# First block's reciprocals over two DMA queues, its second norm by DMA transpose, denominators of three blocks in one visit, and a new order

## The chip, the cores and the metric

The kernel runs on one core of a Trainium2 chip. The metric is the device time of one execution in microseconds (us). The core's engines run side by side, each in the order of its own instruction stream: TensorE (PE, matmuls, with its weight loads shown as PEld), VectorE (DVE), ScalarE (ACT), GpSimd (POOL) and SyncE (SP, which here issues DMAs). They wait for each other through semaphores.

## The reference

One transformer block on x of 2048 rows by 512 columns, bfloat16, without biases: a pre-norm linear attention with 32 heads of width 16, then a pre-norm MLP of width 1792 with ReLU.

```python
qkv = (layernorm(x) @ wqkv) split into q, k, v by head
phi = lambda t: where(t > 0, t + 1, exp(t)) + 1e-6
kv  = sum over s of phi(k)[s, d] * v[s, e]
z   = sum over s of phi(k)[s, d]
o   = (phi(q) @ kv) / (phi(q) @ z + 1e-6)
h   = x + o @ wo
out = h + relu(layernorm(h) @ w1) @ w2
```

## The kernel before, in words

Rows come in 16 tiles of 128 (index t, 0 to 15) and four blocks of four tiles (index c; "block 1" in this text is c = 0). Nothing is scheduled by a tool: `ORDER` is one long string of words, and the program reads it from left to right and records each word's instructions. So each engine's stream is the sequence of that engine's words, and only data and buffers make one engine wait for another. The eight PSUM banks are assigned in the words: in most of them the number behind the indices of the work is the bank.

The words that this text uses, with the engine of each:

- SP: `lx`, `lk`, `lq`, `lv`, `lo`, `l1`, `l2` load x, the three parts of wqkv, wo, w1 and w2; `X` and `x` turn a normalised tile by DMA transpose into lnT (first norm and second norm); `wb` writes a block's reciprocals to HBM (scr), and eight `rb` read them back spread over the partitions (rr); `fd` stores an output tile.
- DVE: `S` and `A` are the statistics of a tile of x, `N` its normalisation; `s`, `a`, `n` the same for h. `M` and `D` finish phi for k (`qM`, `qD` for q). `zc`, `zh` prepare z; `kx` masks kv; `mD` copies half of M (kv times wo) out of PSUM; `dm` multiplies phi(q) by the reciprocals; `hD` adds x; `pD` is the ReLU of two p blocks; `fo` finishes an output tile.
- ACT: `R` and `r` are the reciprocal deviations, `E` the copy of a tile turned by PE, `F` and `U` the exp and the ReLU of k (`qF`, `qU` of q), `gA` and `mA` copy the other halves of G and M, `dl4` and `dx4` take log and exp of the denominators (a reciprocal), `nA` normalises a tile of h.
- PE: `T` and `t` turn a tile by four transposes; `K`, `Q`, `G`, `h`, `p` are blocks of four 512-column matmuls; `ph` is half a p block; `kv` and `m` are small products; `d4` makes a block's denominators with four matmuls, one for each 32 partitions of a bank; `f` is half of the 14 matmuls of an output tile; `z` sums phi(k).

k and q come first (K and Q while x arrives), then G = x-norm times phi(k), which uses banks 4 to 7, then kv and M, and then for each block: denominators, `dm`, h, second norm, p, f. Tiles 0 to 4 of the first norm are turned by PE (`T`, `E`), the others by SP (`X`). In the second norm, tiles 2 and 3 are turned by PE (`t`, then a copy `v` on DVE), the others by SP (`x`).

Lines of the profile that matter: L214 to L220 loads, L248 to L262 statistics and norm, L287 transposes on PE, L297 `E`, L308 and L309 DMA transposes, L316 K, L324 Q, L334 and L337 exp and ReLU, L406 `gA`, L422 `kx`, L440 denominators, L471 spreads, L484 `dm`, L493 h, L508 and L517 p, L537 f.

Of the kernel before, what the change touches and what calls it, by code (L numbers as in the profile page):

```python
# [15 lines left out]


ORDER = """
table const masks warm.70.7.64 warm.2.7 lx.0.1 S.0 A.0 R.0.1 lx.1.1 S.1 lx.2.1 A.1 N.0 T.0.1 lk.0.4 S.2 R.1.1
N.1 T.1.2 lx.3.1 A.2 E.0 K.0.4 R.2.1 lx.4.2 S.3 N.2 T.2.1 E.1 A.3 S.5 R.3.1 K.1.0.0.2 K.1.0.2.2 N.3 S.4 A.5 A.4  # L20
E.2 T.3.2 K.2.6.0.2 K.2.6.2.2 F.0.1 M.0.1 lx.6.2 E.3 S.7 lq.0.4 R.4.2 lx.8.4 Q.0.3.1 N.4 U.0.1 A.7 F.1.1 F.2.1
T.4.2 N.5 S.6 Q.0.1.4 U.1.1 M.1.1 A.6 lx.12.4 M.2.1 D.0.1 R.6.2 K.3.7.0.2 K.3.7.2.2 E.4 X.5 U.2.1 U.3.1 D.1.1
N.6 Q.0.0.3 N.7 S.10 qF.0.0.2 K.4.5 K.5.6 S.8 A.10 S.9 A.8 qU.0.0.2 S.12 F.4.2 D.2.1 X.6 Q.0.2.0 A.9 A.12 K.6.2
S.13 S.11 M.4.2 A.11 A.13 U.4.2 D.4.2 F.3.1 R.8.2 N.9 M.3.1 X.7 K.7.3 R.12.2 R.10.2 N.8 F.6.2 D.3.1 N.13 S.15
G.0 G.1 U.6.2 S.14 X.9 X.8 N.10 A.14 A.15 N.12 qM.0.0.2 M.6.2 X.13 qF.0.2.2 R.14.2 qU.0.2.2 qM.0.2.2 N.11 G.2
G.3 G.5 G.4 N.14 X.12 K.9.3 K.8.2 K.13.1 N.15 qD.0.0.2 D.6.2 za.4.1 X.11 X.10 F.8.2 U.8.2 M.8.2 K.12.0 U.12.2
F.12.2 G.7 za.6.0 K.11.3 D.8.2 qD.0.2.2 M.12.2 za.8.0 K.10.2 F.10.2 X.14 G.8 K.14.0 U.10.2 X.15 K.15.1 M.10.2 zf
lv.2.2 lv.0.2 G.9 D.10.2 zhi D.12.2 F.14.2 G.6 G.10 G.11 M.14.2 zlo U.14.2 D.14.2 z.0.0 z.2.0 z.3.0 z.1.0 G.14
lo.0.2 lo.2.2 zc zh d4.0.1 dl4.0 l1.0.2 G.13 G.12 G.15 dx4.0 gA.2.2 Q.1.1.3 Q.1.0.2 qF.1.0.2 gD.0.2 kv.1.4
kv.3.4 kv.0.4 kv.2.4 kx qU.1.0.2 qM.1.0.2 qD.1.0.2 Q.1.3.1 Q.1.2.0 qF.1.2.2 m.0.2 m.1.3 mD.0.2 m.3.7 m.2.6 wb.0  # L30
Q.2.0.4 Q.2.1.5 rb.0.7 rb.0.1 rb.0.6 rb.0.3 rb.0.0 rb.0.2 rb.0.4 rb.0.5 l1.2.2 qM.1.2.2 qU.1.2.2 Q.2.3.1
qD.1.2.2 mA.2.2 qF.2.0.2 Q.2.2.0 qU.2.0.2 dm.0.2.2 dm.0.0.2 qM.2.0.2 h.1.6 hD.1 s.1 a.1 qU.2.2.2 d4.1.3 dl4.1
h.0.7 hD.0 s.0 dx4.1 h.2.6 h.3.5 a.0 l2.0.7 wb.1 hD.2 nA.1 hD.3 qF.2.2.2 nA.0 s.2 s.3 Q.3.0.2 Q.3.1.3 a.2
Q.3.3.6 a.3 qF.3.0.2 qU.3.0.2 Q.3.2.5 x.1 r.0.4 qF.3.2.2 n.2 t.2.7 n.3 t.3.4 qD.2.0.2 v.2 v.3 x.0 ph.0.3.1.0
ph.0.1.3.0 ph.0.2.0.0 ph.0.3.1.1 qM.2.2.2 qM.3.0.2 ph.0.0.2.0 ph.0.0.2.1 qM.3.2.2 qD.3.0.2 qU.3.2.2 qD.2.2.2
ph.0.2.0.1 qD.3.2.2 p.0.7.5 d4.2.6.2 pD.0.2.2 dl4.2 dl4.3 rb.1.4 rb.1.6 rb.1.3 rb.1.2 rb.1.0 rb.1.1 ph.0.1.3.1
rb.1.7 rb.1.5 p.0.6.4 dx4.2 dm.1.0.2 dm.1.2.2 h.4.0 pD.0.0.2 hD.4 pD.0.6.2 p.0.5.1 h.6.6 dx4.3 p.0.4.0 hD.6
l2.7.7 h.5.4 pA.0.4.2 s.4 s.6 hD.5 h.7.7 a.4 a.6 p.0.11.6 p.0.10.5 s.5 hD.7 a.5 p.0.9.4 wb.2 rb.2.6 n.4 rb.2.0
rb.2.4 s.7 n.6 rb.2.3 rb.2.2 rb.2.1 a.7 n.5 n.7 rb.2.5 rb.2.7 dm.2.0.2 dm.2.2.2 pD.0.10.2 p.0.13.1 p.0.12.0
p.0.8.3 pD.0.12.2 wb.3 r.4.4 rb.3.0 rb.3.4 h.10.7 hD.10 x.6 h.8.2 h.11.6 hD.8 s.10 rb.3.5 rb.3.1 rb.3.6  # L40
f.1.0.0.7 rb.3.3 rb.3.2 rb.3.7 s.8 hD.11 pD.0.8.2 h.9.5 f.3.1.0.7 x.7 x.5 s.11 a.8 hD.9 f.1.0.7.7 f.0.4.0.7 a.10
a.11 x.4 dm.3.2.2 dm.3.0.2 h.14.7 h.12.3 s.9 n.11 h.15.6 a.9 n.10 h.13.2 fo.1 n.9 n.8 hD.14 s.14 hD.12 x.11
hD.15 f.0.4.7.7 r.8.4 p.1.13.7 p.1.6.3 a.14 hD.13 s.12 s.15 s.13 a.12 a.15 a.13 n.14 p.1.12.6 n.13 f.3.1.7.7
n.12 n.15 p.1.2.5 fo.0 pD.1.12.2 x.10 p.1.7.4 fo.3 p.1.3.6 x.9 pD.1.6.2 pD.1.2.2 r.12.4 x.8 p.1.11.2 p.1.10.1
pD.1.10.2 f.2.4.0.7 p.2.0.6 p.2.1.7 f.2.4.7.7 pD.2.0.2 p.2.10.0 p.2.11.1 fo.2 x.14 p.2.6.2 p.2.7.3 x.15 fd.3
p.2.13.7 p.2.12.6 pD.2.10.2 pD.2.6.2 x.12 fd.1 pD.2.12.2 p.2.2.0 x.13 fd.0 p.2.3.1 p.1.5.6 p.1.4.5 pD.2.2.2
pD.1.4.2 p.1.0.3 p.1.1.4 p.1.9.1 p.1.8.0 pD.1.0.2 pD.1.8.2 f.4.4.0.7 f.4.4.7.7 fo.4 fd.4 f.5.3.0.7 f.5.3.7.7
fo.5 fd.2 f.6.7.0.7 f.6.7.7.7 fo.6 p.2.4.2 p.2.5.3 f.7.0.0.7 f.7.0.7.7 pD.2.4.2 fo.7 p.3.6.1 p.3.7.2 pD.3.6.2
p.3.8.3 p.3.9.4 p.3.5.1 pD.3.8.2 p.3.4.0 pD.3.4.2 fd.6 p.3.10.3 p.3.11.4 pD.3.10.2 p.3.2.0 p.3.3.1 p.3.0.5
p.3.1.6 pD.3.2.2 pD.3.0.2 p.3.13.3 fd.7 p.3.12.2 pD.3.12.2 f.10.1.0.7 f.15.2.0.14.3.1 f.15.7.0.14.0.2 p.2.8.4  # L50
p.2.9.5 fo.15.3.1 fd.15.3.1 fo.15.0.2 pD.2.8.2 f.8.7.0.7 f.10.1.7.7 fo.10 f.8.7.7.7 fo.8 f.14.2.0.7 f.14.2.7.7
f.13.3.0.7 fd.5 fd.8 fd.10 fo.14 f.13.3.7.7 fo.13 f.9.0.0.7 f.9.0.7.7 fd.15.0.2 f.11.6.0.7 f.11.6.7.7 fd.13 fo.9
f.12.0.0.7 fd.9 f.12.0.7.7 fo.11 fd.14 fd.11 fo.12 fd.12 f.15.2.0.14.2.1 fo.15.2.1 fd.15.2.1
"""


# [1 line left out]
def kernel(  # L58
# [10 lines left out]
    nc = tc.nc  # L69
# [3 lines left out]
    S, D = xf.shape  # L73
# [7 lines left out]
    KD = D // P  # L81
    KF = FF // P
# [5 lines left out]
    const = ctx.enter_context(tc.tile_pool(name="const", bufs=1))  # L88
# [58 lines left out]
    rb = big.tile([P, NE, 2, CW], BF16, name="rb")  # L147
# [10 lines left out]
    def pk(t, n=1):  # L158
        return pk_lo[:, t : t + n, :] if t < 2 else acts[0][:, t - 2 : t - 2 + n, :]
# [9 lines left out]
    z_on = lambda n: z_sb.rearrange("p (k o) -> p k o", o=1).broadcast_to([P, KD, n])  # L169
    at_bank = {}  # L170
    summed, stated = set(), set()
    dsts = {"k": lambda t, n: pk(t, n), "q": lambda i, n: pqT[i // KD][:, i % KD : i % KD + n, :]}
    unit = {"k": 0, "q": NT}

# [137 lines left out]
    def op_K(t, b, k=0, n=KD):  # L312
        c, j = divmod(t, CT)
        at_bank["k", t] = b
        for kd in range(k, k + n):
            nc.tensor.matmul(  # L316
                bk[:, b, :], lhsT=lnT[c][:, kd, j * P : (j + 1) * P], rhs=wk_sb[:, kd, :],
                start=(kd == 0), stop=(kd == KD - 1),
            )

    def op_Q(c, j, b):
# [145 lines left out]
    def op_wb(c):  # L467
        nc.sync.dma_start(out=scr[c].rearrange("j h o n -> (j h) (o n)"), in_=rd[:, c, :])

    def op_rb(c, h):  # L470
        nc.sync.dma_start(  # L471
            out=rr[h * DH : (h + 1) * DH, :, :],
            in_=scr[c][:, h, :, :].rearrange("j o n -> o j n").broadcast_to([DH, KD, CW]),
        )

    def op_rs(c, j):
        rows = rd[j * Q4 : j * Q4 + P // DH, c, :]
        nc.sync.dma_start(
            out=rr[:, j, :], in_=rows.rearrange("h (o n) -> h o n", o=1).broadcast_to([P // DH, DH, CW])
        )  # L480
# [52 lines left out]
    def op_f(t, b, f0, n, k=0, w=KD):  # L533
        c, j = divmod(t, CT)
        at_bank["f", t, k] = b
        for f in range(f0, f0 + n):
            nc.tensor.matmul(  # L537
                bk[:, b, 0 : w * P], lhsT=acts[c % 2][:, f, j * P : (j + 1) * P],
                rhs=w2_sb[:, f, k * P : (k + w) * P],
                start=(f == 0), stop=(f == KF - 1),  # L540
            )

    def op_fo(t, k=0, w=KD):
# [44 lines left out]
```

## Time and profile before

| What | Value |
|---|---|
| Median of 3 runs | 169.78 us (169.41 to 170.17) |
| Profiled execution, span from first to last instruction | 168.0 us |
| What the median has beyond that span | 1.8 us |
| PE busy | 162.7 us (97%) |
| DVE, ACT, POOL busy | 115.6, 49.5, 4.8 us |
| Granted TensorE clock | 1.00 |
| DMA, mean | 95 GB/s |

The profile gives no other time of the profiled execution than its span; it starts with the program's first instruction and ends with its last, and what the runs' times have beyond it is launch and end. Busy is the time in which an engine works; matmuls are pipelined, so that the length of a single one, or of a short group, contains about 0.17 us of draining that the next one overlaps. A row of the timeline gives start, length, engine, line, operation, what is written and read, and in brackets the idle time of the engine ahead of it with what ended it. A row of SP is the issue of a DMA alone: its data moves later.

### The profile page before, as it was taken

What the parts mean: (1) busy time and instruction counts of PE and PEld (TensorE: products, weight loads), DVE (VectorE), ACT (ScalarE), POOL (GpSimd) and SP (SyncE); (2) the same over time, 40 slices, a digit from 0 to 9 for tenths busy, and PEclk for the clock granted to TensorE, in tenths of its full rate; (3) what the DMA queues carried; (4) which work ended last, traced back from release to release, by engine and by line L of the source; (5) the groups of instructions that cost most, each with busy time, mean ns of one, the idle gap of its engine ahead of it and who ended that gap; (6) DMA issues with size and microseconds to landing.
All of it is one profiled execution on the core that took longest, in us unless ns stands there. A gap on an engine that the chain in (4) does not pass through costs nothing.

```text
span 168.0 us, 2417 instructions
## 1 busy us (share of the span) xinstructions
PE 162.7 (97%) x924; PEld 79.2 (47%) x924; DVE 115.6 (69%) x217; ACT 49.5 (29%) x83; POOL 4.8 (3%) x21
## 2 busy tenths in 40 slices
PE   7799999999999999999999999999999999999992
PEld 7444444454544754444444444444444447444442
DVE  3899999942579999999999755764144773432312
ACT  3799968715798843100101000000000000000000
POOL 7400000000000000000000000000000000000000
PEclk9999999999999999999999999999999999999999
DMA  4984054681595364414552520000101000011021
GB/s 108 353 298 88 20 106 95 189 301 45 132 337 161 98 205 132 132 48 123 83 102 57 126 63 0 0 0 0 62 31 35 0 0 7 32 34 48 31 94 39
DMA packets 25003, 16.01 MB, mean 95 GB/s; under 512 B 15008, under 2 KB 23968, under 8 KB 24992
## 3 DMA queue, kind: packets, MB, share of 16 engines
q1 hardware_dynamic: 24992, 15.87, 33.2%
q8 instruction: 7, 0.11, 0.3%
q14 instruction: 4, 0.03, 0.1%
HBM read 9.96 MB, written 2.62 MB: 75 GB/s over the span
## 4 chain that ended last, share of the span: by engine, by line
PE 92%; DMA 4%; SPq 2%; DVE 1%; issue 0%
PE bk L537 28%; PE bk L508 27%; PE bk L324 8%; PE bk L368 8%; PE bk L493 8%; PE bk L316 7%; DMA wq_sb<-in_A_wqkv_dram 4%; PE bk L517 2%; SPq L214 2%; PE bk L440 1%; DVE gT L545 1%; PE bk L392 1%; PE bk L414 1%; PE bk L426 1%; PE bk L287 0%
## 5 line engine op out<-in xcount | busy, mean ns | idle before, releaser
L537 PE MATMUL bk<-w_sb,at 128*128 128x512 bf16 (+2 forms) x252 | 50.0, 355 | 0.0
L508 PE MATMUL bk<-lnT,w_sb 128*128 128x512 bf16 x208 | 46.9, 379 | 0.0
L528 DVE TENSOR_SCALAR at<-bk 128x1024 bf16<-128x1024 f32 x27 | 32.8, 1223 | 13.2 <-PE bk L508 13.2
L537 PEld LDWEIGHTS <-at 128*128 128x128 bf16 x252 | 23.5, 98 | 25.4
L508 PEld LDWEIGHTS <-w_sb 128*128 128x128 bf16 x208 | 20.4, 98 | 23.9
L545 DVE SCALAR_TENSOR_TENSOR gT<-bk,rstd,h_nat 128x512 bf16<-128x512 f32 (+2 forms) x18 | 12.4, 691 | 24.6 <-PE bk L537 22.0
L334 ACT ACTIVATE eb<-bk 128x1024 bf16<-128x1024 f32 (+1 forms) x18 | 16.6, 929 | 5.3 <-PE bk L316 2.8
L337 ACT ACTIVATE rb<-bk 128x1024 bf16<-128x1024 f32 (+1 forms) x18 | 16.4, 929 | 0.0
L324 PE MATMUL bk<-lnT,wq_sb 128*128 128x512 bf16 x64 | 15.1, 379 | 0.3 <-DMA wq_sb<-in_A_wqkv_dram 0.3
L316 PE MATMUL bk<-wk_sb,lnT 128*128 128x512 bf16 x64 | 15.3, 379 | 0.0
L493 PE MATMUL bk<-m_sb,pqs 128*128 128x512 bf16 x64 | 15.1, 379 | 0.0
L368 PE MATMUL bk<-at,h_nat 128*128 128x512 bf16 x56 | 13.1, 379 | 0.0
L248 DVE BATCH_NORM_STATS2 st<-x_nat 128x6 f32<-128x512 bf16 x16 | 10.6, 678 | 2.3 <-DMA x_nat<-in_A_x_dram 2.3
L499 DVE TENSOR_TENSOR h_nat<-bk,x_nat 128x512 bf16<-128x512 f32 x16 | 10.6, 676 | 0.9 <-PE bk L493 0.9
L254 ACT ACTIVATE rstd<-mv,eps 128x2 f32<-128x2 f32 (+2 forms) x14 | 4.2, 297 | 23.7 <-DVE mv L251 20.9
L250 DVE BATCH_NORM_STATS2 st<-h_nat 128x6 f32<-128x512 bf16 x16 | 10.5, 684 | 0.1
L324 PEld LDWEIGHTS <-wq_sb 128*128 128x128 bf16 x64 | 6.1, 98 | 7.7 <-DMA wq_sb<-in_A_wqkv_dram 0.8
L493 PEld LDWEIGHTS <-pqs 128*128 128x128 bf16 x64 | 6.1, 98 | 7.7 <-DVE pqs L484 0.6
L368 PEld LDWEIGHTS <-h_nat 128*128 128x128 bf16 x64 | 6.1, 98 | 7.3 <-issue 0.2
L316 PEld LDWEIGHTS <-lnT 128*128 128x128 bf16 x64 | 6.1, 98 | 6.8
L341 DVE TENSOR_SCALAR eb<-eb 128x1024 bf16<-128x1024 bf16 (+1 forms) x18 | 6.6, 389 | 0.0
L262 DVE TENSOR_SCALAR h_nat<-x_nat,mv,rstd 128x512 bf16<-128x512 bf16 x16 | 6.3, 408 | 0.2 <-ACT rstd L255 0.2
(65 smaller groups left out, 87.7 us busy)
## 6 DMA issues: line engine op xcount, KB each, us to landing
w_sb<-in_B_w_dram SPq DMA_DIRECT2D x4, 896.0 KB, 6.2
rr<-scr SPq DMA_DIRECT2D x32, 64.0 KB, 2.6
out_dram<-gT SPq DMA_DIRECT2D x15, 128.0 KB, 1.9
x_nat<-in_A_x_dram SPq DMA_DIRECT2D x2, 512.0 KB, 7.9
x_nat<-in_A_x_dram SPq DMA_DIRECT2D x4, 128.0 KB, 2.2
wk_sb<-in_A_wqkv_dram SPq DMA_DIRECT2D x1, 512.0 KB, 4.1
x_nat<-in_A_x_dram SPq DMA_DIRECT2D x2, 256.0 KB, 4.6
wq_sb<-in_A_wqkv_dram SPq DMA_DIRECT2D x1, 512.0 KB, 6.2
```

The costliest lines, as they stand in the source:

```text
L248: op_S = lambda t: nc.vector.bn_stats(out=st[:, t, :], in_=x_nat[:, t, :])
L316: nc.tensor.matmul(bk[:, b, :], lhsT=lnT[c][:, kd, j * P : (j + 1) * P], rhs=wk_sb[:, kd, :], start=(kd == 0), stop=(kd == KD - 1),)
L324: nc.tensor.matmul(bk[:, b, :], lhsT=wq_sb[:, kd, j * P : (j + 1) * P], rhs=lnT[c][:, kd, :], start=(kd == 0), stop=(kd == KD - 1),)
L334: nc.scalar.activation(out=buf(eb, kind, i, n), in_=bank(at_bank[kind, i], n), func=ACT.Exp)
L337: nc.scalar.activation(out=buf(rb, kind, i, n), in_=bank(at_bank[kind, i], n), func=ACT.Relu)
L368: nc.tensor.matmul(bk[:, KD + kd, :], lhsT=ln_nat[:, t, kd * P : (kd + 1) * P], rhs=pk(t)[:, 0, :], start=(not stated), stop=(len(stated) ...
L493: nc.tensor.matmul(bk[:, b, :], lhsT=pqs[:, (c * KD + jb) % NQ, j * P : (j + 1) * P], rhs=m_sb[:, jb, :], start=(jb == 0), stop=(jb == KD ...
L499: nc.vector.tensor_tensor(out=h_nat[:, t : t + n, :], in0=bank(at_bank["h", t], n), in1=x_nat[:, t : t + n, :], op=ALU.add,)
L508: nc.tensor.matmul(bk[:, b, :], lhsT=w1_sb[:, kd, f * P : (f + 1) * P], rhs=lnT[c][:, kd, :], start=(kd == 0), stop=(kd == KD - 1),)
L528: nc.vector.tensor_scalar(out=acts[c % 2][:, f : f + n, :], in0=bank(at_bank["p", c, f], n), scalar1=-1.0, scalar2=0.0, op0=ALU.mult, op1= ...
L537: nc.tensor.matmul(bk[:, b, 0 : w * P], lhsT=acts[c % 2][:, f, j * P : (j + 1) * P], rhs=w2_sb[:, f, k * P : (k + w) * P], start=(f == 0), ...
L545: nc.vector.scalar_tensor_tensor(out=o_t[:, t % NO, cols], in0=bk[:, at_bank["f", t, k], 0 : w * P], scalar=rstd2[:, t : t + 1], in1=h_nat ...
```

## The change

Three things are done differently, and the whole order is new.

- A new word `ab` issues a spread of reciprocals from ACT's queue instead of SP's. Four of the eight spreads of block 1 use it.
- Tiles 2 and 3 of the second norm are turned by DMA (`x.2`, `x.3`) instead of PE and DVE (`t`, `v`).
- One `d4` makes the denominators of blocks 2, 3 and 4 in three banks, where one made those of block 2 and a later one those of blocks 3 and 4.
- A counter (`part`) sets start and stop flags of accumulations, so that halves of K and f may come in either order.

The new order also moves words on every engine. Ahead of the first Q there are now four K blocks instead of three. Half of wv, half of wo and half of w2 are loaded much earlier, half of wo and half of w1 later.

```diff
-table const masks warm.70.7.64 warm.2.7 lx.0.1 S.0 A.0 R.0.1 lx.1.1 S.1 lx.2.1 A.1 N.0 T.0.1 lk.0.4 S.2 R.1.1
...
+table const lx.0.1 warm.70.7.64 lx.1.1 masks lx.2.1 lk.0.4 lx.3.1 S.0 lx.4.2 S.1 lx.6.2 lq.0.4 A.0 warm.2.7 A.1
...
+    fed = {}
+
+    def part(key, n):
+        at = fed[key] = fed.get(key, 0) + 1
+        return {"start": at == 1, "stop": at == n}
...
 def op_K:
-                start=(kd == 0), stop=(kd == KD - 1),
+                **part(("k", t), KD),
...
-    def op_rb(c, h):
-        nc.sync.dma_start(
+    def spread(eng, c, h):
+        eng.dma_start(
             out=rr[h * DH : (h + 1) * DH, :, :],
             in_=scr[c][:, h, :, :].rearrange("j o n -> o j n").broadcast_to([DH, KD, CW]),
         )
+
+    op_rb = lambda c, h: spread(nc.sync, c, h)
+    op_ab = lambda c, h: spread(nc.scalar, c, h)
...
 def op_f:
-                start=(f == 0), stop=(f == KF - 1),
+                **part(("f", t, k), KF),
```

Three places of the new order follow, each before and after. In the listings the lines are those of the file in question (L248 before is L253 after), and the numbers behind a name tell buffers apart.

DVE in the head, before: BN_STATS is `S`, BN_AGGR `A`, TENSOR_SCALAR into h_nat `N`; the rows begin with `S.2`.

```order
L248 BN_STATS st<-x_nat 128x6
L262 TENSOR_SCALAR h_nat<-x_nat,mv,rstd 128x512
L249 BN_AGGR mv<-st 128x2
L248 BN_STATS st<-x_nat 128x6
L262 TENSOR_SCALAR h_nat<-x_nat,mv,rstd 128x512
L249 BN_AGGR mv<-st 128x2
```

The same place after, again from `S.2`:

```order
L253 BN_STATS st<-x_nat 128x6
L267 TENSOR_SCALAR h_nat<-x_nat,mv,rstd 128x512
L254 BN_AGGR mv<-st 128x2
L267 TENSOR_SCALAR h_nat<-x_nat,mv,rstd 128x512 x2
L253 BN_STATS st<-x_nat 128x6
L254 BN_AGGR mv<-st 128x2
```

Before, `N.2` (the second TENSOR_SCALAR) stood behind `S.3`; now `N.1` and `N.2` come together, and `S.3` behind them.

SP between the last loads of x and those of the weights, before: lnT with the number 86 belongs to block 2, 87 to block 3, 88 to block 4.

```order
L214 DMA x_nat<-in_A_x_dram 128x2048 x2
L308 DMA_TRANSPOSE lnT_86<-h_nat 128x4x128 x3
L308 DMA_TRANSPOSE lnT_87<-h_nat 128x4x128 x2
L308 DMA_TRANSPOSE lnT_88<-h_nat 128x4x128 x2
L308 DMA_TRANSPOSE lnT_87<-h_nat 128x4x128 x2
L308 DMA_TRANSPOSE lnT_88<-h_nat 128x4x128 x2
L220 DMA wv_sb<-in_A_wqkv_dram 128x2x512 x2
```

SP at the same place, after:

```order
L219 DMA x_nat<-in_A_x_dram 128x2048 x2
L313 DMA_TRANSPOSE lnT_86<-h_nat 128x4x128 x3
L225 DMA wv_sb<-in_A_wqkv_dram 128x2x512
L225 DMA wo_sb<-in_A_wo_dram 128x2x512
L225 DMA w_sb<-in_B_w_dram 128x7x512
L313 DMA_TRANSPOSE lnT_87<-h_nat 128x4x128 x2
L313 DMA_TRANSPOSE lnT_88<-h_nat 128x4x128 x2
```

Three loads, the last of them seven of the fourteen slices of w2, moved in between the third and the fourth transpose (`X.6` and `X.8`). The three transposes of block 2 are those of tiles 5, 6, 7 before and 5, 7, 6 after.

ACT from the reciprocals of block 1 on, before: ld and rd are `dl4.0` and `dx4.0`, gT `gA`, eb and rb `qF.1.0`, `qU.1.0` and then `qF.1.2`.

```order
L446 ACTIVATE ld<-bk,eps_78 128x512
L451 ACTIVATE rd<-ld 128x512
L406 ACTIVATE gT<-bk 128x1024
L334 ACTIVATE eb<-bk 128x1024
L337 ACTIVATE rb<-bk 128x1024
L334 ACTIVATE eb<-bk 128x1024
```

ACT at the same place, after, where m_sb is `mA`:

```order
L451 ACTIVATE ld<-bk,eps_78 128x512
L456 ACTIVATE rd<-ld 128x512
L411 ACTIVATE gT<-bk 128x1024
L476 DMA rr<-scr_114 16x4x512 x4
L339 ACTIVATE eb<-bk 128x1024
L342 ACTIVATE rb<-bk 128x1024
L434 ACTIVATE m_sb<-bk 128x1024
L339 ACTIVATE eb<-bk 128x1024
```

The four issues of spreads now stand ahead of the exp and the ReLU of the first half of block 2's q.

## What I predicted, before any run of the changed kernel

> **What bounds the kernel now.** I read the page first (span and busy shares), then one long window, the chain that ended last, and the timeline and waits of the places that the new order touches.
>
> ```profile
> span 168.0 us, 2417 instructions
> ...
> PE 162.7 (97%) x924; PEld 79.2 (47%) x924; DVE 115.6 (69%) x217; ACT 49.5 (29%) x83; POOL 4.8 (3%) x21
> ```
> ```profile
> 10.40:164.20 153.80, 153.80 (x814) 73.13 (x815) 107.39 (x192) 43.07 (x67) 0.00 (x0) 1.00 0.31 85
> ```
>
> The columns of the second view are the stretch, its length, the busy time of PE, PEld, DVE, ACT and POOL, the TensorE clock, the DMA share and GB/s. From 10.4 to 164.2 us PE has no idle moment, at a granted clock of 1.00. So three things can be won: PE work that disappears, the ten microseconds ahead of this stretch, and the 3.8 us behind it. Any new wait of PE in between is lost in full. The span is 1.78 us under the runs' median of 169.78; I carry that difference over.
>
> The chain gives the price of PE work (start, length, group, matmuls):
>
> ```profile
> 50.23 0.33 PE bk L440 x4
> ...
> 56.70 0.45 PE bk L287 x8
> ...
> 61.07 0.55 PE bk L440 x8
> ...
> 101.01 12.09 PE bk L508 x56
> ```
>
> A 512-column matmul costs 12.09 / 56 = 0.216 us, so a block of four (a K, Q, G, h or p) costs 0.865.
>
> **The change, part by part.**
>
> *PE work removed.* The transposes `t.2` and `t.3` are the 0.45 row: gain 0.45. The denominators cost 0.33 for block 1, 0.33 for block 2 and 0.55 for blocks 3 and 4. In the row of 0.55 the second group of four added 0.22 to the first, so one visit for blocks 2 to 4 should cost 0.77 in place of 0.88: gain 0.11. The other PE words only change places.
>
> *The head.* Here PE is short of work. First DVE, then PE, then ACT's copy `E.3`:
>
> ```profile
> 6.62 0.69 DVE L248 BATCH_NORM_STATS2 st<-x_nat 128x6 f32<-128x512 bf16 x1 [0.51 <-DMA x_nat<-in_A_x_dram]
> 7.23 0.40 DVE L262 TENSOR_SCALAR h_nat<-x_nat,mv,rstd 128x512 bf16<-128x512 bf16 x1
> 7.54 0.17 DVE L249 BATCH_NORM_AGGREGATE mv<-st 128x2 f32<-128x6 f32 x1
> ```
> ```profile
> 6.32 1.03 PE L316 MATMUL bk<-wk_sb,lnT 128*128 128x512 bf16 x4
> 7.68 0.40 PE L287 MATMUL bk<-ident,h_nat 128*128 128x128 bf16 x4 [0.34 <-DVE h_nat L262]
> 7.92 1.03 PE L316 MATMUL bk<-wk_sb,lnT 128*128 128x512 bf16 x4
> 8.79 0.40 PE L287 MATMUL bk<-ident,h_nat 128*128 128x128 bf16 x4
> 9.02 1.03 PE L316 MATMUL bk<-wk_sb,lnT 128*128 128x512 bf16 x4
> 10.38 0.39 PE L324 MATMUL bk<-lnT,wq_sb 128*128 128x512 bf16 x1 [0.33 <-DMA wq_sb<-in_A_wqkv_dram]
> ```
> ```profile
> 9.22 0.60 ACT L297 ACTIVATE lnT<-bk 128x512 bf16<-128x512 bf16 x1
> ```
>
> Before, `K.1` waits until 7.92 because `T.2` stands ahead of it, `T.2` waits for `N.2`, and `N.2` stands on DVE behind `S.3`, which waited for tile 3 to land. `K.2` is issued by 9.02 + 0.865 = 9.88, and the first Q waits for wq until 10.38. After, `N.2` is ahead of `S.3`, and `K.3` ahead of the first Q. `S.1` now precedes `A.0`, so everything of tile 0 comes up to one S (0.69) later; I take `K.0` at 6.8 instead of 6.32. From there PE has `K.0`, `K.1`, `T.3`, `K.2`, `K.3`: 4 x 0.865 + 0.22 = 3.68, to 10.5, past the landing of wq. `K.3` needs `E.3` by 9.65: it ended at 9.82 before, and `A.3` no longer waits 0.22 behind `N.2`, so 9.60, just in time. At 10.5 PE has one K more done than before at 10.38: 0.865 - 0.13 = 0.73 won, or 0.5 if `E.3` still ends at 9.82.
>
> Part of it goes back at `K.6`, whose tile comes by a DMA transpose from SP:
>
> ```profile
> 11.10 1.83 SPq L308 DMA_TRANSPOSE lnT<-h_nat  x1
> 13.15 1.19 SPq L308 DMA_TRANSPOSE lnT<-h_nat  x1
> 14.44 1.22 SPq L308 DMA_TRANSPOSE lnT<-h_nat  x1
> ...
> DMA to landing us min/median/max: 2.4/2.4/3.4
> ```
> ```profile
> 11.59 0.28 DVE L341 TENSOR_SCALAR eb<-eb 128x512 bf16<-128x512 bf16 x1
> ...
> 12.05 0.75 DVE L344 TENSOR_TENSOR pk_lo<-rb,eb 128x512 bf16<-128x512 bf16 x2
> ```
>
> A transpose costs SP 1.2 and starts every 1.3 us; it lands 2.4 after its issue. In the new order `N.5` has `S.6`, `M.1` and `D.0` more ahead of it on DVE and `N.2` and `N.4` less: 0.69 + 0.28 + 0.37 - 0.80 = 0.54. So `X.5` is issued near 11.7, and tile 6 comes third instead of second: 11.7 + 2 x 1.3 + 2.4 = 16.7 at the least, 17.35 if the first takes 1.83 again. PE reaches `K.6` at 10.5 + 7 x 0.865 + 0.22 = 16.78. Cost 0 to 0.6; I take 0.45, since the first transpose's row is the nearest. So PE starts G near 10.5 + 8 x 0.865 + 0.22 + 0.45 = 18.1, against 10.38 + 9 x 0.865 + 0.22 = 18.38 before: net 0.28.
>
> *Loads ahead of `X.8`.* Half of wv, half of wo and half of w2 (256 + 256 + 896 KB) now stand on SP between `X.6` and `X.8`.
>
> ```profile
> 46.50:51.50 5.00, 5.00 (x27) 2.06 (x25) 4.01 (x8) 4.97 (x7) 0.00 (x0) 1.00 1.00 357
> 61.50:64.80 3.30, 3.30 (x21) 1.60 (x18) 3.10 (x5) 2.26 (x4) 0.00 (x0) 1.00 0.83 287
> ```
>
> At these rates (last column) the 1.44 MB take 4.0 to 5.0 us. Issued near 16.0, with 1.2 until they move (an estimate: half of a transpose's landing), they end at 21.2 to 22.3. `X.8` goes out near 19.2, about as before; behind them it lands near 22 to 22.9. PE wants it for `K.8`, after `K.6` and six G: 17.2 + 7 x 0.865 = 23.3. Hidden, so I cost it at nothing. The lower end of this is no gain, the upper one is a rival.
>
> *Spreads on two queues.* Four of eight spreads of block 1 go to ACT, between `gA` and `qF.1.0`:
>
> ```profile
> 41.17 3.62 SPq L471 DMA_DIRECT2D rr<-scr  x8
> 44.83 0.94 SPq L220 DMA_DIRECT2D w_sb<-in_B_w_dram  x2
> ```
> ```profile
> 40.73 1.02 ACT L406 ACTIVATE gT<-bk 128x1024 bf16<-128x1024 f32 x1 [1.33 <-PE bk L368]
> 42.46 1.02 ACT L334 ACTIVATE eb<-bk 128x1024 bf16<-128x1024 f32 x1 [0.70 <-PE bk L324]
> 43.38 1.02 ACT L337 ACTIVATE rb<-bk 128x1024 bf16<-128x1024 f32 x1
> ```
> ```profile
> DVE pqs L484 <- DMA rr<-scr: 0.2, 1, 0.2
> ```
> ```profile
> 43.35 0.69 DVE L422 TENSOR_TENSOR kvbd<-bk,mask 128x512 bf16<-128x512 f32 x1 [1.82 <-PE bk L414]
> ```
>
> Eight spreads took SP 3.62, or 0.46 each. DVE waited for them only 0.2, and in the new order the multiplication that uses them stands behind the copy of M: an earlier landing buys nothing. The cost is on ACT, 4 x 0.46 = 1.84 at SP's price. Behind them `qF.1.0` and `qU.1.0` empty banks 2 and 3, and `Q.2.1` writes bank 2. Counted from the end of PE's issue of the last G: `gA` starts at 0.2, its successor 0.92 later (42.46 to 43.38), then four issues to 2.96, `qF` 0.92, `qU` 1.02 and a handover, 4.95. PE meanwhile has `Q.1.0`, `Q.1.1`, four kv groups (0.22 each), `Q.1.3`, four m, `Q.1.2`: 5 x 0.865 + 0.89 = 5.21. ACT has 0.26 to spare, 0.07 per issue. No row shows an issue on ACT. SP's copies of 64 and of 896 KB (0.46, 0.47) are the nearest, so I take 0; a transpose's 1.2, the farthest, would make 4 x 1.2 - 1.84 - 0.26 = 2.7. Besides, only one Q now covers `kx`: drain 0.17 + 0.69 + handovers 0.07 = 0.93 against 0.865, cost 0.07.
>
> *Tiles 2 and 3 by DMA.* The new transposes follow those of tiles 1 and 0 on SP.
>
> ```profile
> 49.20 1.03 PE L493 MATMUL bk<-m_sb,pqs 128*128 128x512 bf16 x4
> 52.68 1.21 SPq L309 DMA_TRANSPOSE lnT<-hn  x1
> ```
>
> Before, tile 1 went out 3.48 after the first h; now `hD.0` stands ahead of `a.1`, so about 4.0. Three more issues at 1.3 and 2.4 to land: tile 2 is there 10.3 after the first h. PE needs it for the second half of `ph.0.1`, after 4 h, 6 Q and 4 half blocks: 10 x 0.865 + 4 x 0.43 = 10.38. Bare cover, cost 0 to 0.6 (one issue of 1.83 among them); I take 0.1.
>
> *The tail* ends on the same words and keeps its 3.8 us.
>
> Sum: 0.28 + 0.45 + 0.11 - 0.07 - 0.1 = 0.67 us won; 169.78 - 0.67 = 169.1.
>
> **Rivals.** *ACT's issues take turns with SP's (slower).* If the two queues can't be served at once, the eight issues still take 8 x 0.46 from the landing of scr, 0.75 after the time zero used above, to 4.45. ACT resumes there, 1.5 late, and `Q.2.1` stalls by 1.5 - 0.26, about 1.2: 170.3. It outweighs the gain once an issue holds ACT for 0.46 + 0.07 + 0.67 / 4 = 0.70. For it: all eight are due at once. Against it: an issue costs the same for 64 and for 896 KB, so what is shared seems small. The Trainium skill, Perfetto Trace Analysis, section "DMA Instruction — HWDGE (DVE, Sync)", says that the descriptor generator is locked for exclusive use until all descriptors are made, and that the wait for the lock is counted in the issuing instruction. By that rule the sum is this rival's 170.3, without it 169.1; no row here can show it, as one queue issued everything.
>
> *The loads hold the transposes' issue.* The 1.83 of `X.5` fell while the last x loads may still have been moving. If that is the cause, `X.8` and `X.9` pay 0.6 each; six transposes follow at 1.3 apiece, with 0.3 of cover, so PE loses 0.9: 170.0. Against it: the second of the two loads in the row of 0.94 was issued behind 896 KB and took no longer.
>
> *More is won.* If `X.6` costs nothing to 0.25 and tile 2 nothing, 168.5 to 168.8.
>
> *The two queues change nothing* is already in the sum, at zero.
>
> **How the numbers follow.** Forecast (168.8 to 169.5) 0.45; more won 0.15; ACT's turns 0.18; held transposes 0.12; both, or a stall I haven't seen, 0.10 (171 and above). Predicted 169.1; the range, without the last case and the far ends, 168.5 to 170.8. A measurement of this kernel can't tell less than about 0.5% (0.85 us) from no change, so faster means under 168.93, slower over 170.63. Faster is "more won" and a little of the forecast, 0.25; slower is the last case and parts of the two losing rivals, 0.22; same 0.53.
>
> **What would show it.** Head: first Q near 10.5 without a wait for wq, then a PE wait of up to 0.6 for a transpose, and G from 18.1. ACT: four issues of about 0.45 and no PE wait before `Q.2.1`; a wait of over 1 us there is the first rival. PE waits for lnT between 23 and 31 us are the second. The prediction is wrong if PE waits over 0.3 us in all after 62 us, where I found each wait of PE covered.

## The result: slower, by a wait and a halved clock

The changed kernel took 174.34 us (median of 4 runs, 173.09 to 174.55) against 169.59 us before: 1.0259 times the time before, 95% interval 1.0233 to 1.0285. Run again in a later set it took 173.06 us against 169.92: 1.0165 (1.0118 to 1.0211). Every ratio in this text is over the runs within 1.5% of the fastest of the kernel, which leaves out two of the six in the later set, those at a mean clock of 0.990. I had forecast 169.1 and a range of 168.5 to 170.8. The execution in the profile took 174.55 us with a span of 172.8, so 1.75 us lie outside the span, as before.

The page of the changed kernel, then its PE waits (microseconds in total, times, longest):

```profile
span 172.8 us, 2378 instructions
...
PE 164.0 (95%) x900; PEld 79.6 (46%) x916; DVE 115.1 (67%) x215; ACT 49.3 (29%) x83; POOL 4.8 (3%) x21
...
PEclk9999996999999999999999999999999999999999
```
```profile
PE bk L321 <- DMA lnT<-h_nat: 2.9, 1, 2.9
...
PE bk L525 <- DMA lnT<-hn: 0.3, 1, 0.3
```

PE has less to do than before and is busy longer. The third row shows why: in the seventh of 40 slices, 25.9 to 30.2 us, the granted clock is 0.6. One wait of 2.9 us stands just ahead of it. L321 is K, and the tile it waits for comes by DMA: it is `K.8` waiting for `X.8`. (16 of the 916 matmuls have no record, which is why PE's count is short and why gaps of 0.05 and a wait on "issue" show up that are none.)

SP's issues in that stretch, and the landing of `X.8` alone (the view of its line, narrowed to its issue):

```profile
11.99 4.10 SPq L313 DMA_TRANSPOSE lnT<-h_nat  x3
16.14 0.57 SPq L225 DMA_DIRECT2D wv_sb<-in_A_wqkv_dram  x1
16.75 0.47 SPq L225 DMA_DIRECT2D wo_sb<-in_A_wo_dram  x1
17.27 0.47 SPq L225 DMA_DIRECT2D w_sb<-in_B_w_dram  x1
19.40 10.81 SPq L313 DMA_TRANSPOSE lnT<-h_nat  x8
```
```profile
DMA to landing us min/median/max: 7.0/7.0/7.0
```

Nothing is late on SP. The eight transposes go out from 19.40 on, as forecast (near 19.2). But `X.8` lands 7.0 us after its issue, at 26.4, where I had 22 to 22.9. The DMA view from 15 to 30 us says what it lands behind (the row of GB/s has 40 slices of 0.375 us; the last row gives KB and the time from issue to landing):

```profile
GB/s 216 28 10 207 133 0 79 85 358 374 366 180 177 188 199 191 199 195 225 247 183 218 216 207 184 120 236 76 8 66 268 246 254 279 243 99 0 181 167 2
...
w_sb<-in_B_w_dram SPq DMA_DIRECT2D x1, 896.0 KB, 7.7
```

The loads ran at 358 to 374 GB/s for 1.1 us, then at about 190 from 19.1 us on. The half of w2 landed at 17.27 + 7.7 = 25.0, and `X.8` 1.4 after it. PE's timeline and its clock around the wait (the clock is the column ahead of the DMA share):

```profile
22.78 0.81 PE L373 MATMUL bk<-at,h_nat 128*128 128x512 bf16 x3
26.47 2.76 PE L321 MATMUL bk<-wk_sb,lnT 128*128 128x512 bf16 x7 [2.89 <-DMA lnT<-h_nat]
29.46 2.33 PE L321 MATMUL bk<-wk_sb,lnT 128*128 128x512 bf16 x8 [0.22 <-issue]
```
```profile
26.40:27.00 0.60, 0.53 (x3) 0.93 1.30 262
27.00:27.50 0.50, 0.50 (x3) 0.50 1.33 263
...
30.00:30.50 0.50, 0.50 (x3) 0.67 0.53 110
30.50:31.00 0.50, 0.50 (x4) 1.00 0.77 152
```

K restarts at full clock; half a microsecond later the clock drops to 0.50 and stays there for 3.4 us. The work lost by that is 0.07 x 0.6 + 0.50 x 3.0 + 0.33 x 0.5 = 1.71 us.

One more reading of this profile, the spreads on ACT and on SP:

```profile
45.83 1.80 ACTq L476 DMA_DIRECT2D rr<-scr  x4
```
```profile
45.82 1.75 SPq L476 DMA_DIRECT2D rr<-scr  x4
```

Four issues take ACT 1.80 and SP 1.75, at the same time: 0.45 each, and no turns to be seen.

### The profile page after: what moved, and what is told of

The parts are those of the page before. It is cut to its first block, busy times and chain, and to the rows that moved or that the text cites. A ratio compares the mean times of both kernels' runs of the same rounds, so it can differ in the third digit from the quotient of the medians.

```text
span 172.8 us, 2378 instructions
## 1 busy us (share of the span) xinstructions
PE 164.0 (95%) x900; PEld 79.6 (46%) x916; DVE 115.1 (67%) x215; ACT 49.3 (29%) x83; POOL 4.8 (3%) x21
## 4 chain that ended last, share of the span: by engine, by line
PE 70%; DVE 13%; DMA 11%; issue 2%; SPq 1%; ACT 1%; ACTq 1%; DVEq 0%
PE bk L545 27%; PE bk L516 26%; PE bk L501 6%; PE bk L321 5%; DVE st L253 4%; DMA lnT<-h_nat 4%; PE bk L373 3%; DMA x_nat<-in_A_x_dram 2%; DMA rr<-scr 2%; DVE h_nat L507 1%; DMA lnT<-hn 1%; DVE st L255 1%; PE bk L525 1%; DVE h_nat L267 1%; DMA scr<-rd 1%
## 5 line engine op out<-in xcount | busy, mean ns | idle before, releaser
L536 DVE TENSOR_SCALAR at<-bk 128x1024 bf16<-128x1024 f32 x27 | 32.1, 1218 | 17.6 <-PE bk L516 16.5
L553 DVE SCALAR_TENSOR_TENSOR gT<-bk,rstd,h_nat 128x512 bf16<-128x512 f32 (+2 forms) x18 | 12.2, 688 | 19.2 <-PE bk L545 17.4
L321 PE MATMUL bk<-wk_sb,lnT 128*128 128x512 bf16 x63 | 16.3, 407 | 3.1 <-DMA lnT<-h_nat 2.9
L253 DVE BATCH_NORM_STATS2 st<-x_nat 128x6 f32<-128x512 bf16 x16 | 10.4, 677 | 2.3 <-DMA x_nat<-in_A_x_dram 2.3
L507 DVE TENSOR_TENSOR h_nat<-bk,x_nat 128x512 bf16<-128x512 f32 x16 | 10.4, 677 | 2.2 <-PE bk L501 2.1
L321 PEld LDWEIGHTS <-lnT 128*128 128x128 bf16 x64 | 6.3, 104 | 12.0 <-DMA lnT<-h_nat 3.9
```

The source lines that it names most:

```text
L253: op_S = lambda t: nc.vector.bn_stats(out=st[:, t, :], in_=x_nat[:, t, :])
L321: nc.tensor.matmul(bk[:, b, :], lhsT=lnT[c][:, kd, j * P : (j + 1) * P], rhs=wk_sb[:, kd, :], **part(("k", t), KD),)
L536: nc.vector.tensor_scalar(out=acts[c % 2][:, f : f + n, :], in0=bank(at_bank["p", c, f], n), scalar1=-1.0, scalar2=0.0, op0=ALU.mult, op1= ...
L553: nc.vector.scalar_tensor_tensor(out=o_t[:, t % NO, cols], in0=bk[:, at_bank["f", t, k], 0 : w * P], scalar=rstd2[:, t : t + 1], in1=h_nat ...
```

## Experiments

All of them are edits of the order. In the experiments' kernels line numbers are one lower than in the changed kernel (K is L320, a DMA transpose of the first norm L312 and of the second L313). They ran in four sets, each beside runs of the kernel before, which scatter from 169.2 to 171.0; the ratio to those, not the median, is what sets are compared by:

| Kernel | Median, us | Ratio | 95% interval |
|---|---|---|---|
| three loads back | 170.39 | 1.0021 | 0.9992 to 1.0051 |
| only w2 back, behind `x.2` | 169.96 | 0.9996 | 0.9964 to 1.0028 |
| changed, 12 matmuls in the wait | 171.73 | 1.0110 | 1.0067 to 1.0153 |
| changed, 6 matmuls in the wait | 171.57 | 1.0087 | 1.0062 to 1.0112 |
| before, with the three loads early | 171.09 | 1.0060 | 1.0033 to 1.0087 |
| w2 behind `wb.1` | 170.44 | 1.0014 | 0.9993 to 1.0035 |
| the same, one queue | 171.05 | 1.0052 | 1.0024 to 1.0080 |
| the same, `t.2`, `t.3` on PE | 169.76 | 1.0003 | 0.9979 to 1.0028 |
| w2 behind `wb.1`, 6 more matmuls at the start | 169.13 | 0.9958 | 0.9939 to 0.9977 |
| the same, one queue | 169.86 | 0.9996 | 0.9978 to 1.0015 |
| the same, `t.2`, `t.3` on PE | 169.93 | 1.0001 | 0.9984 to 1.0018 |

### Are the early loads the cause, and which?

```diff
-A.9 D.2.1 lv.0.2 S.8 K.7.3 F.4.2 lo.2.2 S.13 l2.7.7 K.6.2
+A.9 D.2.1 S.8 K.7.3 F.4.2 S.13 K.6.2
...
-lv.2.2 K.15.1
+lv.2.2 lv.0.2 K.15.1
...
-lo.0.2 Q.1.0.2
+lo.0.2 lo.2.2 Q.1.0.2
...
-x.2 Q.3.2.0
+x.2 l2.7.7 Q.3.2.0
```

> The changed kernel with the three early loads moved back on SP's queue: half of wv behind its other half, half of wo behind its other half, half of w2 behind x.2. Theory (the loads stand ahead of X.8 in the data, so X.8 lands 3.0 us after PE wants it, and the wait then halves the TensorE clock for some 3.4 us, which costs 1.7 more): both go, 4.7 of the difference; what is left is what else the change won and lost, so 169.3 to 170.0, X.8 landing 2.4 after its issue and a granted clock of 1.00 between 23 and 32 us. Rival (the eight transposes are late for another reason, such as their new order or their issue): 173 to 174.5, the wait before K.8 stays.

The second kernel moves only `l2.7.7`, to the same place.

> The changed kernel with only the half of w2 (896 KB) moved back behind x.2; the halves of wv and wo (512 KB) stay ahead of X.8. Theory (what counts is how much data is still to be moved when X.8 is issued): the 512 KB were in at 19.9, X.8 is issued at 19.4 and lands by 22.4, an us before K.8 wants it at 23.4: no wait, no clock drop, as with all three moved back (169.3 to 170.0). Rival (any load issued ahead slows the transposes that follow, since it makes their descriptors or their issue late): X.8 lands at 23.5 to 25, PE waits 0.5 to 1.5 us: 170.5 to 172.5.

Both bring the time back to that of the kernel before. With only w2 moved, 512 KB still stand ahead of `X.8`, and PE runs from G (L372, which ends the row ahead) into K (L320) without a gap:

```profile
20.63 2.75 PE L372 MATMUL bk<-at,h_nat 128*128 128x512 bf16 x12
23.23 3.61 PE L320 MATMUL bk<-wk_sb,lnT 128*128 128x512 bf16 x16
```
```profile
DMA to landing us min/median/max: 3.4/3.4/3.4
```

`X.8` lands 3.4 after its issue at 19.20, at 22.6. So without the 896 KB neither the order of the transposes, their issue nor the 512 KB does harm, and both rivals fall; whether the 896 KB alone would do it, without the 512 KB ahead of them, no run shows. The second kernel's time is as expected, at the slow end; the first one's is 0.4 above. What is left of the change seems to win nothing, which the next sections take up.

The first kernel also showed a side effect that I hadn't thought of. Its profiled execution (its longest, 172.1 us) has these rows, of ACT's issues and of PE's waits:

```profile
41.56 3.14 ACTq L475 DMA_DIRECT2D rr<-scr  x4
```
```profile
PE bk L328 <- ACT rb L341: 0.7, 1, 0.7
```

In the trace the DMAs mark their completion on eight semaphores in turn. With `lo.2.2` put in ahead of the spreads, the last spread on ACT stands eight places behind it and has the same semaphore; it went out at 44.40, `lo.2.2` had landed at 44.38. So an issue seems to wait until the DMA eight places earlier has landed: ACT's four issues last 3.14 instead of 1.80, and 0.7 of it reaches PE. How much of this the 1.0021 contains isn't shown, since only this one execution was profiled.

### The wait and the clock taken apart

```diff
-G.5 X.12 S.14 K.8.2
+G.5 X.12 S.14 warm.12.2.512 K.8.2
```

> The changed kernel with twelve more matmuls of 512 columns on zeros in bank 2 just ahead of K.8 (2.6 us of work in the 3.0 us wait; K.8 overwrites them). Theory (the wait for X.8 costs 3.0 by itself, and 1.7 more because TensorE's clock is halved behind it): K.8 starts when it did, at 26.5, but at a granted clock of 1.00: 1.4 to 1.7 us faster than the changed kernel, 172.6 to 173.0. Rival (the lower clock comes from something else, such as the eight transposes that land at once, or has no part in the loss): 174.0 to 174.6 and the clock at 0.5 from 27 to 30 us as before.

> The changed kernel, its three early loads where the change put them, with six matmuls of 512 columns on zeros ahead of K.8 (1.3 us; twelve of them, 2.6 us, gave 171.7). Theory (a wait of PE of about 3 us, not the late transposes as such, halves the clock): PE idles 0.2 to 1.8 us, by when X.8 lands, at a clock of 1.00: 170.9 to 173.0, and below 172.2 only if X.8 lands before 25.5. Rival (any wait for X.8 brings the clock down, or the landing of the transposes does): a clock of 0.5 for some 3 us behind the wait, 173.0 to 174.6.

The second kernel has six matmuls there instead of twelve. Of the one with twelve, then of the one with six:

```profile
23.07 2.75 PE L249 MATMUL bk<-m_sb 128*128 128x512 bf16 x12
25.66 3.62 PE L320 MATMUL bk<-wk_sb,lnT 128*128 128x512 bf16 x16
```
```profile
22.98 1.46 PE L249 MATMUL bk<-m_sb 128*128 128x512 bf16 x6
25.83 3.63 PE L320 MATMUL bk<-wk_sb,lnT 128*128 128x512 bf16 x16 [1.40 <-DMA lnT<-h_nat]
```
With 1.4 us of idleness left, and with none, sixteen matmuls of K take 3.6 us (16 x 0.216 and the drain): full clock, although the transposes land just as late and as closely together. So the idle PE brings the clock down. By the ratios both kernels are 1.5% and 1.7% faster than the changed one in its first set, 2.5 and 2.9 us, where I had expected 1.4 to 1.7 with twelve matmuls (against its later set 0.55% and 0.78%); and the one with six is below 172.2 although `X.8` landed at 25.8 in its profile, against what I wrote. What I had left out is that the head and the wait for `x.2` differ too: in the profile with six matmuls G starts at 17.8 instead of 18.25, and PE doesn't wait for `x.2`.

The changed kernel once more:

> The changed kernel itself once more, beside the kernel before on this chip. Theory (a wait of 2 to 3 us for X.8, and 1.7 us more when it halves TensorE's clock): two groups, one near 174.3 at a mean clock of 0.99, one 1.1 to 1.7 us lower at a clock of 1.00; the lower by how late X.8 lands, which was 24.9 to 26.4 so far. Rival (the clock has no part in it): the times do not go with the clock.

Its six runs, time and mean clock:

```
171.97 1.000   172.02 1.000   172.99 0.998   173.14 0.999   174.95 0.990   174.97 0.990
```

The first set had 174.20, 174.48 and 174.55 at 0.990 and 173.09 at 0.998. So the times do go with the clock: at 0.99, 174.2 to 175.0; else 172.0 to 173.1. Halved for 3.4 us, the mean over 172.8 us is 0.990, as shown. The profile this time is of one of the lower runs (172.02):

```profile
24.99 3.63 PE L320 MATMUL bk<-wk_sb,lnT 128*128 128x512 bf16 x16 [1.91 <-DMA lnT<-h_nat]
```
A wait of 1.9 left the clock alone, one of 2.9 halved it. No run was profiled that waited in between, so where the limit lies is open. The Trainium skill, TensorE: Matmul & The Clock Gate, Part 1, has the clock fall to half after an idle window of about 3.4 us, and its windows run freely, whatever the kernel does; in its closing table it warns of gaps above about 3 us. The half clock and the 3.4 us for which it lasted agree; here a gap of 2.9 was enough, and no run shows where the windows stand.

### The loads alone, in the old order

```diff
-S.14 X.9 X.8
+S.14 lv.0.2 lo.2.2 l2.7.7 X.9 X.8
```

(and the three words taken out where they stood.)

> The kernel before with one part of the change alone: half of wv, half of wo and half of w2 moved ahead of X.9, the first transpose of the second group. Theory: X.9 lands at 25 to 26.5 in place of 21.8, PE wants it at 23.6: a wait of 1.5 to 3 us and then, where the wait is near 3, the clock drop of 1.7 as well: 171.2 to 174.5. Rival (the loads are harmless in this order, and the loss needs the rest of the change): 169.3 to 170.2.

1.0060, some 1.0 us: slower, and with a median of 171.09 just under what I expected. The loads do harm by themselves, but `X.9` landed at 24.4 in its profile, and PE waited 0.3 for it there. One of its twelve runs had a mean clock of 0.99; it took 173.81, the other eleven 170.2 to 171.5. So this one move lies near the edge: in the old order it mostly costs an us, in the new one, where `X.8` landed at 24.9 to 26.4 in four profiles, 1.5 to 3 us and often the clock too.

The load is not what spreads these four landings: it took 7.5 to 7.7 us in each. `X.8` landed 0.5 behind it in two of them and 1.5 in the other two. In all four a fetch of 8 KB of instructions (queue q14) was under way at the same time. From 21.5 to 25.5 us, first in the changed kernel's first profile, then in its second:

```profile
q14 instruction: 1, 0.01, 4.5%
```
```profile
q14 instruction: 1, 0.01, 2.2%
```

4.5% and 2.2% of 16 engines for 4.0 us are 2.9 and 1.4 us. In the two profiles with 1.5 us the fetch ended 0.15 after the load had landed, in the two with 0.5 about 1.0 before it. Of the changed kernel's two waits, 2.89 and 1.91, nearly the whole difference is that `X.8` landed 1.48 behind the load in one and 0.54 in the other, so a fetch may have decided whether the clock fell. The next section shows what a fetch does to a transpose; for this place no run separates it.

### What ate the rest: an instruction fetch

The kernel with only w2 moved back had a second wait:

```profile
PE bk L524 <- DMA lnT<-hn: 0.8, 1, 0.8
```
```profile
DMA to landing us min/median/max: 3.5/3.5/3.5
```

It is `x.2` (the second row is its landing, 3.5 us after its issue). I took the 896 KB, now right behind it, for the reason, and moved them on behind `wb.1`.

> The changed kernel with the half of w2 behind wb.1, the writing out of the denominators of block 2, instead of ahead of X.8; the halves of wv and wo stay where the change put them. With the half of w2 right behind x.2, x.2 landed 3.46 us after its issue and PE waited 0.81 for it. Theory (that load slowed x.2; nothing else is wrong with the second norm by DMA): x.2 lands 2.4 after its issue, the wait falls to 0 to 0.3: 169.0 to 169.5. Rival (the fourth transpose in a row is too late whatever stands behind it): the wait stays at 0.6 or more, 169.8 to 170.2.

The theory fell: 1.0014, and `x.2` late again. The DMA view of that kernel from 55.4 us (just ahead of the issue of `x.2` at 55.5) to 59.1, where it lands; 40 slices of 0.09 us:

```profile
GB/s 111 210 208 227 221 210 166 51 6 0 0 0 177 0 91 213 213 205 205 199 152 37 9 3 8 6 11 8 11 8 8 11 20 0 0 0 0 0 0 0
...
q8 instruction: 1, 0.02, 1.8%
```

The first hump is `x.3`. Then, in the single slice of 177, one packet of queue q8: 16 KB of instructions. Then the hump of `x.2`, some 0.7 us long like the other; but behind it 8 to 11 GB/s go on for another us. A hump at 210 GB/s over 16 DMA engines is 13 for each, so the tail fits one engine that is late, by about the time that the fetch took (1.8% of 16 engines for 3.7 us, 1.1). In the trace each DMA reports its landing in sixteen steps, and `x.2` counts as landed with the last. In all fourteen profiles, wherever a DMA transpose with no load of x or of weights still in flight ahead of it landed in more than 2.7 us (31 times), a fetch lay in its time of flight. The reverse depends on the moment: where the fetch began 0.7 to 2.0 us after the issue, the transpose was late each time; where it began in the last 0.25 us before the landing, or one of 8 KB within 0.65 us of the issue, it landed in 2.4 to 2.6. `X.5` of the kernel before (3.4) and `X.8` of the kernel with w2 moved back (3.4, a fetch of 8 KB) had a fetch beside them too, though loads as well. In the changed kernel's first profile the fetch of 16 KB fell beside `x.1`, in its second beside `x.2`; in the two with matmuls in the wait for `X.8` it came 6 us earlier, and `x.2` landed in 2.4. So I put six more of the small matmuls at the very start, where PE waits for the first tile, to change nothing but the place of the fetch:

```diff
-table const lx.0.1 warm.70.7.64 lx.1.1
+table const lx.0.1 warm.76.7.64 lx.1.1
```

> The kernel with the half of w2 behind wb.1 and 76 instead of 70 small matmuls on zeros at the very start, where PE waits for the first tile anyway. In the runs where x.2 landed 3.5 to 4.0 us after its issue, 16 KB of instructions were fetched by DMA (queue q8) while it was under way; in those that had six or twelve more matmuls ahead of K.8 the fetch came 6 us earlier and x.2 landed in 2.4. Theory (one DMA engine has the fetch to do and brings its part of the transpose an us late): the fetch comes before x.1 is issued, x.2 lands in 2.4, PE does not wait for it: 0.6 to 1.0 us faster than without the six matmuls, 0.4% to 0.6% faster than the kernel before. Rival (the fetch beside the transpose is a coincidence; x.2 is late for what stands ahead of it): x.2 lands in 3.5 again, no change against the kernel before.

The view of the same stretch, 54.8 (where `x.2` is issued) to 58.4:

```profile
GB/s 205 225 210 219 222 191 80 12 0 0 0 0 0 26 145 225 202 230 222 205 159 41 3 0 0 0 0 0 0 0 0 0 0 0 0 0 0 0 0 0
...
lnT<-hn SPq DMA_TRANSPOSE x1, 2.4
```
```profile
10.40:163.40 153.00, 153.00 (x810) 72.73 (x808) 106.79 (x191) 42.10 (x66) 0.00 (x0) 1.00 0.33 87
```

No fetch, no tail, landed in 2.4, and (last row, columns as in the prediction) PE without an idle moment from 10.4 to 163.4 us, in a span of 167.0. 169.13 us, 0.9958 (0.9939 to 0.9977): faster than both kernels, and the time that I had forecast for the whole change. The rival (a coincidence) falls. Nor do the six matmuls show a gain by anything else: with tiles 2 and 3 on PE, where there is no `x.2` to meet the fetch, the kernel is at 1.0003 without them and at 1.0001 with them (the table's two rows with `t.2`, `t.3` on PE). Why six matmuls more bring that fetch 6 us forward, the traces don't say.

The Trainium skill, Runtime: NRT & Kernel Launch, section "Instruction fetch mechanics", says that instructions come in blocks of 16 KiB by the engine's own DMA queue, at a cost that is mostly hidden. The 16 KB agree; the fetches of 8 KB on q14 are another size. Among PE's waits none is for instructions; the cost fell on the DMA transpose beside the fetch, 1.0 to 1.6 us late.

### The parts of the change, priced

First beside the kernel with w2 behind `wb.1`:

> The kernel of the run above with all eight spreads of block 1 on SP's queue, as before the change. Theory (ACT's four issues take 0.45 each beside SP's and lie within PE's work of 5.2 us): within 0.3 us of the run above, either way; ACT's gap of 1.7 us ahead of qF.1.0 is gone and PE waits for it neither with nor without. Rival (the issues on ACT cost PE time ahead of Q.2.1): 0.3 to 1.2 us faster than the run above.

> The kernel two runs above (half of w2 behind wb.1) with the second norm's tiles 2 and 3 transposed by TensorE again and copied by DVE. Theory (the DMA transposes save the two transposes' 0.45 and cost a wait of at most 0.3): 0.2 to 0.45 us slower than with DMA, 169.4 to 169.9. Rival (the wait for x.2 eats all the gain): as fast or up to 0.5 us faster than with DMA.

By these, one queue is slower by 0.4%, against both the theory and the rival, and PE's transposes are as fast as DMA's, as the rival had it. But the first still has the fetch beside `x.2` and the second has no `x.2` at all, so each compares the part together with the fetch. The same two edits once more, with the fetch out of the way:

```diff
-rb.0.4 Q.1.1.3 ab.0.3 rb.0.6 ab.0.1 rb.0.0 ... ab.0.5 rb.0.2 ... ab.0.7
+rb.0.4 Q.1.1.3 rb.0.3 rb.0.6 rb.0.1 rb.0.0 ... rb.0.5 rb.0.2 ... rb.0.7
```

> The fastest kernel so far (half of w2 behind wb.1, 76 matmuls at the start) with all eight spreads on SP's queue. Here no fetch falls beside x.2, so the queues can be compared alone. Theory (ACT's issues cost and win nothing): within 0.3 us of 169.13, 0.2% to 0.6% faster than the kernel before. Rival (eight issues on SP make the spreads land 1.8 us later than two queues do, and DVE, then PE, waits for them): 0.3 to 0.8 us slower than with two queues.

```diff
-x.3 Q.3.3.1 a.2 n.2 qF.2.2.2 qD.1.2.2 x.2 Q.3.2.0 qM.3.0.2
+Q.3.3.1 t.3.3 a.2 n.2 v.3 qF.2.2.2 qD.1.2.2 Q.3.2.0 t.2.2 v.2 qM.3.0.2
```

> The fastest kernel so far with the second norm's tiles 2 and 3 transposed by TensorE again, copied by DVE. Theory (with no fetch beside x.2 the DMA transposes save 0.45 and cost no wait): 0.3 to 0.6 us slower than 169.13, within 0.3% of the kernel before. Rival (PE's transposes stand where PE would wait for something else, so that nothing is saved): within 0.15 us of 169.13.

Against 0.9958 both ratios are 0.4% worse, some 0.7 us, and the intervals do not overlap. One queue, SP's issues, and waits of DVE and PE:

```profile
40.73 3.62 SPq L475 DMA_DIRECT2D rr<-scr  x8
```
```profile
DVE pqs L491 <- DMA rr<-scr: 0.7, 1, 0.7
PE bk L524 <- DMA lnT<-hn: 0.4, 1, 0.4
```

Eight issues on one queue take 3.62 instead of 1.75, `dm` waits 0.7 for the last spread, what follows on DVE is later, and `x.2` with it. The rival holds. Tiles 2 and 3 on PE, then the same place of the kernel with DMA:

```profile
56.08 3.66 PE L524 MATMUL bk<-lnT,w_sb 128*128 128x256 bf16 x32
59.67 1.30 PE L444 MATMUL bk<-pqT,zhd 128*32 128x512 bf16 x12
60.90 1.47 PE L515 MATMUL bk<-lnT,w_sb 128*128 128x512 bf16 x6
```
```profile
55.61 3.66 PE L524 MATMUL bk<-lnT,w_sb 128*128 128x256 bf16 x32
59.20 0.83 PE L444 MATMUL bk<-pqT,zhd 128*32 128x512 bf16 x12
59.96 3.41 PE L515 MATMUL bk<-lnT,w_sb 128*128 128x512 bf16 x15
```

The two transposes make the half blocks start 0.47 later, as costed. Besides, the denominators take 60.90 - 59.67 = 1.23 instead of 0.76: DVE, with the two copies `v` (0.42 each) among its work, ends its last product for q at 60.52, behind their start, where with DMA it ends at 58.91, ahead of it. The theory holds; the gain of 0.7 is more than the expected 0.3 to 0.6.

## Why the prediction was wrong, point by point

Stage by stage, the changed kernel against the one at 169.13 (starts of groups in the two timelines, the last row the spans):

```profile
18.25 1.03 PE L373 MATMUL bk<-at,h_nat 128*128 128x512 bf16 x4
...
45.15 1.89 PE L329 MATMUL bk<-lnT,wq_sb 128*128 128x512 bf16 x8
...
60.81 1.91 PE L525 MATMUL bk<-lnT,w_sb 128*128 128x256 bf16 x16
```
```profile
17.76 1.03 PE L372 MATMUL bk<-at,h_nat 128*128 128x512 bf16 x4
...
22.97 3.40 PE L320 MATMUL bk<-wk_sb,lnT 128*128 128x512 bf16 x15
...
39.94 1.89 PE L328 MATMUL bk<-lnT,wq_sb 128*128 128x512 bf16 x8
```

| Stage begins | Changed | 169.13 | Lost in the stage ahead |
|---|---|---|---|
| G | 18.25 | 17.76 | 0.49, all in the head, where loads came later in this execution (wk by 0.5) |
| `K.8` | 26.47 | 22.97 | 3.01: the wait for `X.8` |
| Q of block 2 | 45.15 | 39.94 | 1.71: the halved clock, as summed above |
| first `ph` | 60.81 | 55.61 | -0.01 |
| end of span | 172.8 | 167.0 | 0.6: the wait for `x.2`, by PE's weight load 0.6 |

- *Loads ahead of `X.8`: "Hidden, so I cost it at nothing."* This step failed, and the result hangs on it. Two assumptions in it fell. First, I reckoned the load's landing from rates of 287 to 357 GB/s, seen in stretches in which SP issued nothing but loads: 4.0 to 5.0 us for all three. w2 alone took 7.7 from its issue, and landed at 25.0 instead of 22.3 at the latest; in the four profiles with these loads it took 7.5 to 7.7. The page of the kernel before had a row that spoke against my sum and that I passed over, the median from issue to landing of its four loads of this size:

```profile
w_sb<-in_B_w_dram SPq DMA_DIRECT2D x4, 896.0 KB, 6.2
```

  From an issue at 17.27 that is 23.5, past the 23.3 at which PE wants `X.8`. Second, I took a margin of 0.4 us between landing and use for enough, though the load's landing was an estimate; `X.8` landed 0.5 to 1.5 after w2.

  The rate of 190 explains the landing only in part. In the second profile of the same kernel (DMA view, again 15 to 30 us) it was back at 289 to 355 from 19.9 to 22.1 us, with transposes being issued as before, and w2 still landed 7.6 after its issue:

```profile
GB/s 2 70 217 63 8 96 208 377 352 320 158 183 216 289 355 341 337 347 299 186 87 41 82 8 22 261 260 243 188 4 93 218 39 7 198 145 0 96 217 37
```

  What holds the landing stays open.
- *The price of a PE wait.* "Any new wait of PE in between is lost in full" was too low. The wait of 2.9 was followed by 1.71 more by the clock. No rival contained this, and the measured time lies in the last case, "a stall I haven't seen", which had no mechanism; "the loads hold the transposes' issue" had the right place and the right wait ("PE waits for lnT between 23 and 31 us") by the wrong mechanism: the issues ran at their 1.2 to 1.3 us, and it was the data that came late.
- *ACT's issues: 0, and no turns taken.* Right: 1.80 beside 1.75. The rival of 170.3 falls, and with it the price that I put on the rule beside it (the Trainium skill, Perfetto Trace Analysis, section "DMA Instruction — HWDGE (DVE, Sync)": an exclusive generator whose lock wait counts in the issue): four issues on each of two queues took no longer than four on one. A lock that is held for less than half of an issue would not show here.
- *"An earlier landing buys nothing."* Wrong in the new order: there the two queues are worth 0.7 us, since `dm` would wait 0.7 for a single one. Against the kernel before, where PE didn't wait for the spreads, they win nothing.
- *Tiles 2 and 3 by DMA: 0.45 won, 0.1 lost.* Right in mechanism; where the fetch keeps away, PE doesn't wait for `x.2`, and without the part the kernel loses 0.7. The bound of "0 to 0.6" for the wait was too narrow: 0.3 to 0.6 in the changed kernel's first profile, 0.8 to 1.3 in those whose fetch fell beside `x.2`, the changed kernel's second (1.1) among them. That a fetch can delay a transfer was missing.
- *One visit for the denominators: 0.11 won; `kx`: 0.07 lost.* The first is right: 0.76 measured, 0.77 costed. The second didn't come: in the kernel at 169.13 PE has no idle moment there.
- *The head: 0.28 won.* Right in direction, somewhat more. wk lands 4.1 us after its issue in the profile before and 4.5 after:

```profile
wk_sb<-in_A_wqkv_dram SPq DMA_DIRECT2D x1, 512.0 KB, 4.5
```

  G starts 18.38 before and 18.25 after, so 0.13 earlier although wk came 0.4 later: about 0.5. The head differs between executions by more than the forecast gain: in the twelve profiles of the new order G starts at 17.7 to 18.7 (median 18.0), in the two of the old order at 18.4 and 18.8. The cost of 0.45 for `X.6` did not come: the first transpose's issue took 1.3, not 1.83.
- *Sum.* With w2 out of the way and the fetch out of the way, the change is worth 0.42% (0.23% to 0.61%), 0.7 us, where the sum said 0.67. That the two agree is in part luck. The two queues and the DMA transposes, each priced by taking it out of the kernel at 169.13, come to 1.4 together, twice the whole: these are prices in the new order, which leans on both, and not gains over the kernel before. Profile against profile (spans 168.0 before, 167.0 at 169.13) the head won 0.62 (0.28 forecast, and subject to the scatter just named) and PE's work 0.55 (0.56 forecast), while 0.21 was lost behind the last matmul, which ends 2.98 ahead of the end before and 3.19 now; the tail, I had said, keeps its time. The 1.44 MB on SP were worth a loss of 3 to 5 us instead of nothing.

## What to carry to other kernels

Here a small transfer issued behind a bulk load on the same queue landed only after the load had, and the loads took some half as long again as I had reckoned from the trace's rates: cost such a move by the longest time from issue to landing that the trace shows for a load of that size, and leave a margin of microseconds, not of tenths. A PE wait that nears 3 us can cost more than its length; here a few matmuls on zeros in it kept the clock. Where a DMA lands late by about an us with nothing else in flight, look for an instruction fetch in that window, and compare orders only in profiles with the fetch in the same place.

## What the runs showed of the hardware that I had not expected

- The TensorE clock fell to 0.50 for 3.4 us after 2.9 us without work, and not after 1.9 or 1.4 us, in one profile each. It fell 0.5 us after the work had resumed.
- The same 896 KB landed 7.5 to 7.7 us after issue in four profiles of the new order with transposes issued behind them, 6.7 in the old order with the loads moved there, and 5.5 in the profile before, at another place. The transposes issued behind a load don't by themselves halve its rate: in the changed kernel's second profile it fell to 158 to 216 GB/s for 1.1 us and was then back at 289 to 355, with transposes still being issued, and the load landed no sooner for it. What holds its landing isn't settled.
- A fetch of 16 KB of instructions made the part of one of the 16 DMA engines of a transpose 1.0 to 1.6 us late: 3.5 to 4.0 instead of 2.4 us to landing. It did so where it began about 1 us after the transpose's issue, and not in every place.
- Issues on ACT and on SP cost 0.45 each at the same time.
